# Decay attention and two feed-forward stages: all attention in float32 matmuls, weights P kept for two units

## The chip, the cores and the metric

The kernel runs on one core of a Trainium2 chip. The metric is the device time of one execution in microseconds (us). Three timed runs of the kernel before gave 955.11, 959.03 and 954.88 us, median 955.11.

## What is computed

Causal attention with a decay (4 batches, 8 heads, 576 positions, head dimension 64), then two feed-forward stages over 2304 tokens of width 512, all in float32 accuracy; the weights of the feed-forward stages come as float64.

```python
scores = scale * q @ k.T
cum = cumsum(log(clip(f, 1e-4, 1)))
scores = where(causal, -1e9, scores + cum[:, None] - cum[None, :])
attn = exp(scores - max); attn /= sum(attn) + 1e-9
x = attn @ v                       # then (tokens, 512)
h = x @ w_in;  h = (h * tanh(softplus(h))) @ w_out
out = max(h @ w1, h @ w2, h @ w3) @ w2_out
```

## The kernel before

**Attention by pairs and units.** Two heads make a pair; the 16 pairs run in order, four to a batch. A pair has two units: g = 0 holds query tiles 0 and 1 (128 rows each, 128 and 256 keys wide), g = 1 tiles 2, 3 (384 and 512 wide) and the last 64 rows of both heads together (tile `q4`, twice 288 wide). For a pair, `prep` turns q and k (PE transposes through PSUM tiles `tr`) into `kT` and `qh`. For a unit, `scores` makes a score tile `sc` by matmul; DVE adds the decay `cb` and takes the minimum (line 476), ACT does exp with the sum (482), DVE and POOL scale by the reciprocal (453 to 456). The result is P. Then `av` turns P, 128 x 128 at a time, into PSUM tiles `pp` (510), copies them to TA or TB, multiplies with v into `av` (532 or 539), and writes the result `xt` to DRAM as `x_d` (570).

**Two ways of multiplying.** `WHOLE = 8` sends pairs 0 to 7 through plain float32 matmuls: a score of one head uses the 64 rows of its head (array mode 64*128; `U` and `L` are the two halves), av writes 64 columns for each head (mode 128*64), and q4's scores and all turns use the whole array (128*128). Float32 matmuls appear in the trace as two records each. Pairs 8 to 15 take the split path: q, k, v and P are split into a high and a low float32r part by DVE, ACT and POOL, both parts stand side by side in the contraction, and every matmul uses mode 128*128, two per product (431, 539); q and k are turned in three versions (362), 27 turns for a pair in place of 10.

**PSUM and P.** `tr`, `sc` and `pp` share four PSUM buffers. P has one buffer per tile name.

**Order.** `attention` emits the scores of a unit, then av of the unit before (`pend`), then prep of the next pair. Between units the main loop emits steps of the first feed-forward layer, `h_steps`: 72 steps, 9 blocks of 256 tokens by 8 column groups, each of 24 float32r matmuls (mm3, lines 188 to 190), at a lower priority. A step needs its block's x: `load_x` reads `x_d` back (213) and POOL splits it into xh and xl (142, 146). A scheduler orders each engine's instructions by priority when the kernel is built; on the chip every engine follows that list. What is left of the steps runs after the attention, and then the next layer (`y`, float32r matmuls with w_out) and the second feed-forward stage.

Of the kernel before, what the change touches and what calls it, by code (L numbers as in the profile page):

```python
# [9 lines left out]
F32 = mybir.dt.float32  # L10
F32R = mybir.dt.float32r
# [22 lines left out]
BLK2 = 512  # L34

WHOLE = 8
# [3 lines left out]
PADS = []  # L40
PART0 = [(1, 256, 0, 256)]
# [28 lines left out]
def tile_decay_attention__mish_ff__max3_ff(  # L70
# [39 lines left out]
    with tc.high_priority(3 * AHEAD):  # L110
        make_identity(nc, ident)
        identr = const.tile([128, 128], F32R, name="identr")
        nc.vector.tensor_copy(identr, ident)
# [120 lines left out]
    raws = [ap_.tile([128, 640 if c == "v" else S], F32, name=f"raw{c}") for c in "qkv"]  # L234


    made_for = {}

    def shared(name, whole):

        if made_for.get(name, (None,))[0] != whole:
            dt = F32 if whole else F32R
            if name[:2] == "vs":
                t = aw.tile([128, 10, 2, 64], dt, name=name)
                if whole:
                    t = t.rearrange("p n a d -> p (n a d)")[:, 0:640]
                    nc.gpsimd.memset(t[U, 512:640], 0.0)
            elif name[:2] == "qk":
                t = ap_.tile([128, 9, 3 - int(name[2]), 64], dt, name=name)
                if whole:  # L250
                    t = t.rearrange("p n a d -> p (n a d)")[:, 0:S]
            elif name[:2] == "q4":
                t = as_.tile([128, 2, 256], dt, name=name)
                if whole:
                    t = t[:, 0, 0:128]
                    nc.gpsimd.memset(t, 0.0)
                else:
                    nc.gpsimd.memset(t[:, :, 64:192].bitcast(F32), 0.0)
            else:
                t = aw.tile([128, 2, 768 if name == "TA" else TBW], dt, name=name)  # L260
            made_for[name] = (whole, t)
        return made_for[name][1]

    for t in sums:
        nc.vector.memset(t, 1.0)
    nc.gpsimd.memset(raws[2][U, 512:640], 0.0)
    count = dict(pair=0, prep=0, unit=0, bank=0)

    def ld(dst, src, b, hp, inner):

        hs = slice(2 * hp, 2 * hp + 2)
        if inner:

            nc.sync.dma_start(
                dst[:, 0:512].rearrange("p (h c) -> p h c", h=2),
                src[b, hs, 0:512, :].rearrange("h (p t) d -> p h (t d)", t=4),
            )
            for h in range(2):
                nc.sync.dma_start(dst[(U, L)[h], 512:S], src[b, 2 * hp + h, 512:S, :])
        else:  # L280
            for h in range(2):
                nc.sync.dma_start(
                    dst[:, h * 256:(h + 1) * 256].rearrange("p (t d) -> p t d", t=4),
                    src[b, 2 * hp + h, 0:512, :].rearrange("(t p) d -> p t d", t=4),
                )
            nc.sync.dma_start(
                dst[L, 512:640].rearrange("p (h d) -> p h d", h=2),
                src[b, hs, 512:S, :].rearrange("h p d -> p h d"),
            )

    def split_raw(t, r, eng="dve"):

        split(t[:, :, 0], t[:, :, 1], r.rearrange("p (n d) -> p n d", d=64), eng, "pool")

    def load(b, hp):

        i = count["pair"]
        count["pair"] += 1
        rq, rk, rv = raws
        whole = i < WHOLE  # L300
        if whole:
            if i % 2:
                rq, rk = (shared(f"qk{n}", True) for n in range(2))
            for dst, src in ((rk, k), (rq, q)):
                for h in range(2):
                    nc.sync.dma_start(
                        dst[:, 0:512].rearrange("p (t h d) -> p t h d", h=2, d=64)[:, :, h],
                        src[b, 2 * hp + h, 0:512, :].rearrange("(t p) d -> p t d", t=4),
                    )
                for h in range(2):  # L310
                    nc.sync.dma_start(dst[(U, L)[h], 512:S], src[b, 2 * hp + h, 512:S, :])
        else:
            ld(rk, k, b, hp, True)
            ld(rq, q, b, hp, True)
# [7 lines left out]
        if not whole:  # L322
            ld(rv, v, b, hp, False)
# [3 lines left out]
        return dict(b=b, hp=hp, cb=(c2, c4), raw=(rq, rk), vs=None if whole else shared(f"vs{i % 2}", False), whole=whole)  # L327
# [24 lines left out]
    def prep(J):  # L352

        raw = raws

        qh = as_.tile([128, 2, 512], F32 if J["whole"] else F32R, name="qh", bufs=2)
        kk = as_.tile([128, 2, S], F32 if J["whole"] else F32R, name="kT", bufs=2)
        last = shared(f"q4{count['prep'] % 2}", J["whole"])
        count["prep"] += 1

        def turn(dst, c, src):
            nc.tensor.transpose(dst[:, c:c + 128].bitcast(F32R), src, identr)

        rest = att_psum("tr")
        if J["whole"]:
            kk, qh = kk[:, 0, :], qh[:, 0, :]
            raw = J["raw"]
            for i, dst in ((1, kk), (0, qh)):
                tr = att_psum("tr")
                for c in range(4):  # L370
                    nc.tensor.transpose(tr[:, c * 128:c * 128 + 128], raw[i][:, c * 128:c * 128 + 128], ident)
                nc.scalar.activation(dst[:, 0:512], tr, AF.Copy)
                nc.tensor.transpose(rest[U, i * 128:i * 128 + 128], raw[i][:, 512:S], ident)
            for h, rows in enumerate((U, L)):
                nc.scalar.activation(kk[rows, 512:S], rest[U, 128 + h * 64:192 + h * 64], AF.Copy)
                nc.scalar.activation(
                    last[rows, h * 64:h * 64 + 64], rest[U, h * 64:h * 64 + 64], AF.Copy
                )
            vs = shared(f"vs{(count['prep'] - 1) % 2}", True)
            ld(vs, v, J["b"], J["hp"], False)  # L380
            J.update(q=qh, q4=last, k=kk, vs=vs)
            mask_decay(J)
            return

        ql = as_.tile([128, 2, 512], F32R, name="ql", bufs=2)
        qk = [shared(f"qk{n}", False) for n in range(2)]
        split_raw(qk[1], raw[1])
        split_raw(qk[0], raw[0])
        nc.gpsimd.tensor_scalar(
            qk[0][:, :, 2], raw[0].rearrange("p (n d) -> p n d", d=64), 1.0, 1.0, op0=ALU.mult, op1=ALU.mult  # L390
        )
        for i, part, dst, n in ((1, 0, kk, 0), (0, 0, qh, 1), (0, 1, ql, 2)):
            src = lambda blk: qk[i][:, blk, part:part + 2, :].rearrange("p a d -> p (a d)")
            for h in range(2):
                tr = att_psum("tr")
                for c in range(4):
                    turn(tr, c * 128, src(4 * h + c))
                nc.scalar.activation(
                    dst[:, h, 0:512].rearrange("p (c t) -> p c t", t=4),
                    tr.rearrange("p (t c) -> p c t", t=4),  # L400
                    AF.Copy,
                )
            turn(rest, n * 128, src(8))
        rr = rest[:, 0:384].rearrange("p (i h c) -> p i h c", i=3, h=2)
        nc.scalar.activation(kk[:, :, 512:S], rr[:, 0], AF.Copy)
        for a in range(2):
            nc.scalar.activation(
                last[:, a].rearrange("p (a c) -> p a c", c=64)[:, 0:4:3, :], rr[:, 1 + a], AF.Copy
            )
        split_raw(J["vs"], raw[2], "act")  # L410
        mask_decay(J)
        J.update(q=(qh, ql), q4=last, k=kk)

    def score_mm(J, h, qt, dst, c0, w):
        if J["whole"]:
            if h is None:
                lhs = J["q4"]
                rhs = J["k"][:, c0:c0 + w]
            else:
                lhs = J["q"][(U, L)[h], qt * 128:qt * 128 + 128]  # L420
                rhs = J["k"][(U, L)[h], c0:c0 + w]
            nc.tensor.matmul(dst, lhs, rhs, start=True, stop=True, skip_group_check=True)  # L422
            return
        if h is None:

# [605 lines left out]
```

## Time and profile before

| | before |
|---|---|
| median of 3 runs | 955.11 us |
| the profiled execution | 956.07 us, its span 954.3 us |
| PE / DVE / ACT / POOL busy | 921.3 / 553.8 / 445.5 / 268.5 us |
| mean granted clock of PE | 0.987 |
| first h matmul, last av | 89.0 us, 384.4 us after the span's start |
| last h matmul | 471.7 us |

Times in the trace count from the span's start. A PE row gives the time from a matmul's start to its result; matmuls overlap, so the distance of starts tells what one costs. A record such as `x8` merges neighbours of one kind. `<-` behind a row names what ended the idle time before it. The granted clock is 1.00 at 2.4 GHz and 0.5 at 1.2 GHz.

### The profile page before, as it was taken

To read this page: it belongs to the slowest core of one execution; us is meant where nothing else is said; L and a number is where in the kernel's file an instruction comes from. 1 tells how busy PE (TensorE), PEld (TensorE's weight loads), DVE (VectorE), ACT (ScalarE), POOL (GpSimd) and SP (SyncE) were. 2 spreads that over 40 slices of the span, in tenths; PEclk is the share of its full clock that TensorE was granted. 3 is DMA by queue.
4 is the path that set the end of the run, shared out by engine and by line. 5 is a ranking of instruction groups with operands and counts; after the bars stand their busy time and mean duration, and the time that the engine had idled before them with its cause. 6 is when DMAs were issued, how large, how long until landed. Compare 5 with 4: busy or idle time off the path is not lost.

```text
span 954.3 us, 15673 instructions
## 1 busy us (share of the span) xinstructions
PE 921.3 (97%) x5480; PEld 789.3 (83%) x5480; DVE 553.8 (58%) x1257; ACT 445.5 (47%) x1003; POOL 268.5 (28%) x353
## 2 busy tenths in 40 slices
PE   6899999999999999899999999999999999999998
PEld 3555677799999999799987878789888999789986
DVE  4457787656665556589146656577684446615440
ACT  5567566666666565433245454554443123412221
POOL 3436666574445621210002000000121233103310
PEclk9889999999999999899999999999999999999999
DMA  7757665554445321867255576665399534334311
GB/s 164 182 143 194 206 184 169 162 154 129 130 136 162 115 69 59 300 207 243 95 181 165 186 224 195 224 213 168 127 308 340 159 115 131 105 100 128 116 32 68
DMA packets 131391, 154.81 MB, mean 162 GB/s; under 512 B 52016, under 2 KB 91440, under 8 KB 131312
## 3 DMA queue, kind: packets, MB, share of 16 engines
q1 hardware_dynamic: 108784, 114.48, 40.6%
q10 hardware_dynamic: 19840, 25.17, 7.4%
q0 software_dynamic: 2688, 14.16, 4.1%
q8 instruction: 43, 0.70, 0.3%
q14 instruction: 36, 0.29, 0.1%
HBM read 107.55 MB, written 46.21 MB: 161 GB/s over the span
## 4 chain that ended last, share of the span: by engine, by line
PE 67%; DMA 15%; DVE 7%; ACT 5%; issue 3%; SPq 1%; POOL 1%; ACTq 0%; POOLq 0%; DVEq 0%
DMA g<-h_d 9%; PE h L189 6%; PE h L190 6%; PE h L188 6%; PE q L189 5%; PE q L190 5%; PE q L188 5%; PE pp L510 4%; PE sc L431 3%; PE av L539 3%; DMA wr<-in_moe_w_in_dram 3%; PE o L188 2%; PE o L189 2%; PE o L190 2%; PE sc L422 2%
## 5 line engine op out<-in xcount | busy, mean ns | idle before, releaser
L188 PE MATMUL h<-xh,wi 128*128 128x256 f32 x576 | 167.5, 291 | 4.0 <-POOL xh L142 2.6
L189 PE MATMUL h<-xl,wi 128*128 128x256 f32 x576 | 166.7, 290 | 1.9 <-POOL xl L146 1.9
L190 PE MATMUL h<-xh,wi 128*128 128x256 f32 x576 | 166.5, 289 | 0.0
L189 PE MATMUL y<-gl,wo 128*128 128x512 f32 (+1 forms) x320 | 118.2, 369 | 0.0
L188 PEld LDWEIGHTS h<-xh,wi 128*128 128x128 f32 x576 | 110.5, 192 | 8.6 <-issue 3.1
L190 PE MATMUL y<-gh,wo 128*128 128x512 f32 (+1 forms) x320 | 117.3, 368 | 0.0
L189 PEld LDWEIGHTS h<-xl,wi 128*128 128x128 f32 x576 | 110.8, 193 | 6.6 <-issue 3.1
L190 PEld LDWEIGHTS h<-xh,wi 128*128 128x128 f32 x576 | 110.8, 192 | 2.9 <-issue 2.2
L188 PE MATMUL y<-gh,wo 128*128 128x512 f32 (+1 forms) x320 | 109.3, 371 | 2.8 <-ACT ze L793 2.5
L765 DVE TENSOR_TENSOR gl<-g,gh 128x512 fp32r<-128x512 f32 x72 | 50.3, 699 | 95.4 <-ACT gh L764 94.8
L758 ACT ACTIVATE g<-g 128x512 f32<-128x512 f32 x72 | 45.3, 631 | 89.2 <-DMA g<-h_d 77.4
L482 ACT ACTIVATE P<-P,mn 128x128 f32<-128x128 f32 (+3 forms) x128 | 71.1, 556 | 32.7 <-DVE mn L476 31.6
L188 PEld LDWEIGHTS y<-gh,wo 128*128 128x128 f32 x320 | 60.1, 188 | 15.1 <-ACT ze L793 4.0
L456 POOL TENSOR_SCALAR P<-P,rr 128x128 f32<-128x128 f32 (+3 forms) x128 | 68.3, 548 | 11.9 <-DVE rr L454 6.5
L189 PEld LDWEIGHTS y<-gl,wo 128*128 128x128 f32 x320 | 60.3, 188 | 11.0 <-DVE gl L765 1.3
L190 PEld LDWEIGHTS y<-gh,wo 128*128 128x128 f32 x320 | 60.2, 189 | 9.8
L510 PE MATMUL pp<-ident,P 128*128 128x128 f32 x320 | 60.9, 295 | 6.2 <-POOL P L456 3.7
L957 DVE TENSOR_TENSOR u<-q,p 128x448 f32<-128x448 f32 x36 | 22.4, 622 | 63.6 <-PE q L190 61.2
L510 PEld LDWEIGHTS pp<-ident,P 128*128 128x128 f32 x320 | 41.2, 150 | 16.9 <-issue 6.5
L853 POOL DMA_DIRECT2D r<-a_d x12 | 6.7, 559 | 161.9 <-ACT b L140 161.6
L764 ACT ACTIVATE gh<-g 128x512 fp32r<-128x512 f32 x72 | 44.7, 620 | 14.3 <-PE y L190 13.6
L177 DVE SCALAR_TENSOR_TENSOR wt<-wr,wt 128x512 int32<-128x512 int32 (+1 forms) x62 | 46.9, 756 | 0.6
(178 smaller groups left out, 2138.4 us busy)
## 6 DMA issues: line engine op xcount, KB each, us to landing
g<-h_d SPq DMA_DIRECT2D x72, 256.0 KB, 3.5
s<-s_d SPq DMA_DIRECT2D x72, 256.0 KB, 2.9
h_d<-he ACTq DMA_DIRECT2D x46, 256.0 KB, 3.2
wr<-in_moe_w_out_dram SPq DMA_DIRECT2D x22, 512.0 KB, 4.5
wr<-in_moe_w_dram SPq DMA_DIRECT2D x24, 384.0 KB, 4.3
s_d<-sk POOLq DMA_DIRECT2D x12, 768.0 KB, 5.0
cb<-cum_d SPq DMA_DIRECT2D x32, 256.0 KB, 4.2
wr<-in_moe_w_in_dram SPq DMA_DIRECT2D x32, 256.0 KB, 3.5
```

Of the source, the lines that this page charges most:

```text
L177: nc.vector.scalar_tensor_tensor(out=ti, in0=lo, scalar=29, in1=ti, op0=ALU.logical_shift_right, op1=ALU.bitwise_or,)
L188: nc.tensor.matmul(ps, wh, xh, start=start, stop=False, skip_group_check=True)
L189: nc.tensor.matmul(ps, wh, xl, start=False, stop=False, skip_group_check=True)
L190: return nc.tensor.matmul(ps, wl, xh, start=False, stop=stop, skip_group_check=True)
L431: nc.tensor.matmul(o, lhs, rhs, start=n == 0, stop=n == len(mms) - 1, skip_group_check=True)
L456: nc.gpsimd.tensor_scalar(made[ci], made[ci], rr[:, ci:ci + 1], 1.0, op0=ALU.mult, op1=ALU.mult)
L482: nc.scalar.activation(Pt, Pt, AF.Exp, scale=-1.0, bias=mn[:, col - 1:col], accum_out=sm[:, ci:ci + 1],)
L510: nc.tensor.transpose(pp[:, n * 128:n * 128 + 128], Pt[:, k0:k0 + 128], ident)
L539: nc.tensor.matmul(avp[h][:, off:off + w], vl, T[:, i, c:c + w], start=kt == 0 and i == 0 and not (g == 0 and h == 1), stop=last and i == ...
L758: nc.scalar.activation(g, g, AF.Mish)
L764: on_act[:] = [nc.scalar.activation(gh, g, AF.Copy)]
L765: on_dve[:] = [nc.vector.tensor_tensor(out=gl, in0=g, in1=gh, op=ALU.subtract)]
```

## The change

- The split path, its identity `identr` and the tiles shared between both paths are gone; all 16 pairs take the plain float32 path.
- P has two buffers (`bufs=LEAD`, 2), and av of a unit follows the scores of two more units: `pend` is a list.
- The score tiles of a unit are issued query tile by query tile, head 0 and head 1 next to each other, instead of head by head.
- q and k have two raw buffers for all pairs, v three.

```diff
-WHOLE = 8
+LEAD = 2
...
+    raws = [[ap_.tile([128, S], F32, name=f"raw{c}{i}") for c in "qk"] for i in range(2)]
+    vs = [aw.tile([128, 640], F32, name=f"vs{i}") for i in range(3)]
...
     def prep(J):
...
+        qq = as_.tile([128, 512], F32, name="qT", bufs=2)
+        kk = as_.tile([128, S], F32, name="kT", bufs=2)
+        last, v_ = q4[J["i"] % 2], vs[J["i"] % 3]
         rest = att_psum("tr")
...
-        split_raw(qk[1], raw[1])
-        split_raw(qk[0], raw[0])
...
-        for i, part, dst, n in ((1, 0, kk, 0), (0, 0, qh, 1), (0, 1, ql, 2)):
...
     def score_mm(J, h, qt, dst, c0, w):
...
-            parts = [(t[:, h, qt * 128:qt * 128 + 128], h) for t in J["q"]]
-        mms = [(ql, J["k"][:, n, c0:c0 + w], dst) for ql, n in parts]
-        for n, (lhs, rhs, o) in enumerate(mms):
-            nc.tensor.matmul(
-                o, lhs, rhs, start=n == 0, stop=n == len(mms) - 1, skip_group_check=True
-            )
+            rows = (U, L)[h]
+            lhs = J["q"][rows, qt * 128:qt * 128 + 128]
+        nc.tensor.matmul(dst, lhs, J["k"][rows, c0:c0 + w], start=True, stop=True, skip_group_check=True)
...
-        tiles += [(h, qt) for h in range(2) for qt in ((0, 1) if g == 0 else (2, 3))]
+        tiles += [(h, qt) for qt in ((0, 1) if g == 0 else (2, 3)) for h in range(2)]
...
-            Pt = aw.tile([128, wd], F32, name=f"P{qt}_{h}")
+            Pt = aw.tile([128, wd], F32, name=f"P{qt}_{h}", bufs=LEAD)
...
-                nc.scalar.activation(T[:, 0, cols], src, AF.Copy)
-                nc.vector.tensor_tensor(out=T[:, 1, cols], in0=src, in1=T[:, 0, cols], op=ALU.subtract)
...
+            if count["bank"] % 2:
+                nc.vector.tensor_copy(T[:, c:c + w], pp[:, :w])
+            else:
+                nc.scalar.activation(T[:, c:c + w], pp[:, :w], AF.Copy)
...
-                vl = J["vs"][:, 4 * h + kt if kt < 4 else 8 + h].rearrange("p a d -> p (a d)")
-                for i in range(2):
...
+                n = 4 * h + kt if kt < 4 else 8 + h
+                nc.tensor.matmul(
+                    acc[(U, L)[h], off:off + w], J["vs"][:, n * 64:n * 64 + 64], T[:, c:c + w],
+                    start=kt == 0, stop=last, skip_group_check=True,
+                )
...
     def attention():
...
+        units = [(ji, g) for ji in range(len(jobs)) for g in range(2)]
+        pend = []
+        for n in range(len(units) + LEAD):
+            if n < len(units):
+                ji, g = units[n]
+                pend.append((J[ji], g, scores(J[ji], g)))
+            if n >= LEAD:
+                unit = pend.pop(0)
+                av(*unit)
...
+            if n < len(units):
+                if g == (ji == 0) and ji + 1 < len(jobs):
+                    prep(J[ji + 1])
+                if g == 1 and ji + 2 < len(jobs):
+                    J[ji + 2] = load(ji + 2, *jobs[ji + 2])
+            yield tok
```

The order of PE before, in the plain pair 1 (mode 64*128 for `qh`; 384 and 512 columns of head 0, then of head 1):

```order
L422 MATMUL sc<-kT,q_372 128x288
L422 MATMUL sc<-kT,qh 128x384
L422 MATMUL sc<-kT,qh 128x512
L422 MATMUL sc<-kT,qh 128x384
L422 MATMUL sc<-kT,qh 128x512
L510 MATMUL pp<-ident,P_0_446 128x128
```

There the four scores stand together. The order of PE before, in a split pair (both parts of one head's score, h matmuls between the heads; all in mode 128*128):

```order
L431 MATMUL sc<-kT,q_2560 128x288 x8
L431 MATMUL sc<-kT,qh 128x384
L431 MATMUL sc<-kT,ql 128x384
L188 MATMUL h<-xh,wi_160 128x256
L189 MATMUL h<-xl,wi_160 128x256
L190 MATMUL h<-xh,wi_160 128x256
L431 MATMUL sc<-kT,qh 128x512
L431 MATMUL sc<-kT,ql 128x512
```

The order of PE after the change, in a pair of the second half (`sc` in mode 64*128, `av` in 128*64, h, lines 184 to 186, in 128*128; a row of `sc` is one head's score):

```order
L324 MATMUL sc<-kT,qT 128x128
L403 MATMUL av<-TB,vs_186 64x320 x2
L184 MATMUL h<-xh,wi_156 128x256
L185 MATMUL h<-xl,wi_156 128x256
L324 MATMUL sc<-kT,qT 128x128
L403 MATMUL av<-TB,vs_186 64x320
L186 MATMUL h<-xh,wi_156 128x256
L324 MATMUL sc<-kT,qT 128x256
L403 MATMUL av<-TB,vs_186 64x320 x2
```

Here the two heads' scores of 128 columns are apart, and the mode changes with nearly every row. Over the whole attention 34 stretches of mode 64*128 and 44 of 128*64 become 87 and 101.

The DMA queue of SP at the attention's end, before (`x_d<-xt` are the last units' results, `xr<-x_d` the reads for the next h block; 66 is block 6):

```order
L570 DMA x_d_66<-xt_5190 128x64
L570 DMA x_d_67<-xt_5190 128x192
L213 DMA xr<-x_d_66 128x1024
L639 DMA h_d_7_92<-he 256x1x256
L570 DMA x_d_67<-xt_5336 128x64
L570 DMA x_d_68<-xt_5336 128x256
```

and after:

```order
L209 DMA xr<-x_d_65 128x1024
L307 DMA vs_185<-in_v_dram 128x4x64 x2
L311 DMA vs_185<-in_v_dram 64x2x64
L417 DMA x_d_67<-xt_4151 128x64
L417 DMA x_d_68<-xt_4151 128x256
L417 DMA x_d_66<-xt_4354 128x64
```

Before, block 6 is read right behind the last write to it, and the PE order has 48 h steps ahead of the last av. After the change block 5 is read ahead of the last fourteen writes, and 30.6 h steps stand ahead of the last av.

## Rows read from the trace of the kernel before

**Rows 1.** The page: span, and busy time of each engine.
```profile
span 954.3 us, 15673 instructions
...
PE 921.3 (97%) x5480; PEld 789.3 (83%) x5480; DVE 553.8 (58%) x1257; ACT 445.5 (47%) x1003; POOL 268.5 (28%) x353
```

**Rows 2.** Busy time by stretch: length, then PE, PEld, DVE, ACT, POOL, clock.
```profile
25.00:50.00 25.00, 22.83 (x117) 12.99 (x117) 10.04 (x37) 14.18 (x44) 9.81 (x21) 0.86 0.68 171
50.00:75.00 25.00, 23.86 (x123) 14.28 (x121) 17.33 (x60) 18.22 (x53) 9.39 (x15) 0.86 0.58 156
75.00:100.00 25.00, 23.61 (x135) 15.47 (x135) 16.61 (x52) 16.87 (x52) 18.87 (x28) 0.93 0.78 222
100.00:175.00 75.00, 72.25 (x465) 51.94 (x464) 60.97 (x133) 46.21 (x119) 44.90 (x52) 1.00 0.60 177
200.00:350.00 150.00, 150.00 (x1266) 148.91 (x1265) 88.68 (x267) 94.52 (x239) 76.41 (x105) 1.00 0.43 130
375.00:400.00 25.00, 20.46 (x148) 20.07 (x147) 10.36 (x20) 11.40 (x20) 7.27 (x5) 0.86 0.69 230
```

**Rows 3.** Busy time of tile h's instructions alone, 200 to 350 us.
```profile
200.00:350.00 150.00, 100.13 (x652) 86.20 (x651) 8.94 (x13) 8.36 (x14) 1.00 0.43 130
```

**Rows 4.** PE in order of time, split path: start us, us, then the group.
```profile
188.74 1.57 PE L362 MATMUL tr<-identr,qk 128*128 128x128 f32 x16
...
193.69 0.69 PE L431 MATMUL sc<-kT,q 128*128 128x288 f32 x4
...
195.56 0.39 PE L431 MATMUL sc<-kT,qh 128*128 128x512 f32 x1
195.80 0.40 PE L431 MATMUL sc<-kT,ql 128*128 128x512 f32 x1
```

**Rows 5.** PE in order of time around the last av.
```profile
382.17 2.52 PE L539 MATMUL av<-TB,vs 128*128 128x320 f32 x17
387.30 0.50 PE L188 MATMUL h<-xh,wi 128*128 128x256 f32 x2 [2.61 <-POOL xh L142]
389.72 0.58 PE L189 MATMUL h<-xl,wi 128*128 128x256 f32 x1 [1.93 <-POOL xl L146]
```

**Rows 6.** PE in order of time, plain path, 101 to 122 us.
```profile
101.13 0.76 PE L532 MATMUL av<-TB,vs 128*64 128x320 f32 x4 [0.70 <-ACT TB L523]
101.82 0.66 PE L371 MATMUL tr<-ident,rawk 128*128 128x128 f32 x4
102.40 0.75 PE L532 MATMUL av<-TB,vs 128*64 128x320 f32 x2
103.08 0.30 PE L373 MATMUL tr<-ident,rawk 128*64 128x128 f32 x1
...
109.03 1.12 PE L422 MATMUL sc<-kT,qh 64*128 64x512 f32 x2
110.08 0.39 PE L188 MATMUL h<-xh,wi 128*128 128x256 f32 x1
110.30 0.28 PE L189 MATMUL h<-xl,wi 128*128 128x256 f32 x1
110.51 0.91 PE L422 MATMUL sc<-kT,qh 64*128 64x384 f32 x2
111.35 0.39 PE L190 MATMUL h<-xh,wi 128*128 128x256 f32 x1
...
121.91 0.60 PE L510 MATMUL pp<-ident,P 128*128 128x128 f32 x4
```

**Rows 7.** PE in order of time, both heads' scores with nothing between them.
```profile
52.37 1.81 PE L422 MATMUL sc<-kT,qh 64*128 64x384 f32 x8
54.13 0.52 PE L510 MATMUL pp<-ident,P 128*128 128x128 f32 x3
```

**Rows 8.** What PE waited for, 12 to 100 us: us in total, times, longest.
```profile
PE pp L510 <- POOL P L456: 3.7, 5, 1.6
```

**Rows 9.** PE in order of time, turns of P in a phase of low clock.
```profile
61.53 1.27 PE L510 MATMUL pp<-ident,P 128*128 128x128 f32 x5
```

More of the change, by code (lines that the diff above doesn't have):

```diff
@@ L264, in tile_decay_attention__mish_ff__max3_ff @@
+    raws = [[ap_.tile([128, S], F32, name=f"raw{c}{i}") for c in "qk"] for i in range(2)]
+    vs = [aw.tile([128, 640], F32, name=f"vs{i}") for i in range(3)]
+    TA = aw.tile([128, 768], F32, name="TA")
+    TB = aw.tile([128, TBW], F32, name="TB")
     for t in sums:
         nc.vector.memset(t, 1.0)
[L266 to L276, printed above, removed]
-            )
-            for h in range(2):
-                nc.sync.dma_start(dst[(U, L)[h], 512:S], src[b, 2 * hp + h, 512:S, :])
-        else:
+    q4 = [as_.tile([128, 128], F32, name=f"q4_{i}") for i in range(2)]
@@ L284, in ld @@
                     src[b, 2 * hp + h, 0:512, :].rearrange("(t p) d -> p t d", t=4),
                 )
[L286 to L314, printed above, removed]
@@ L315, in load @@
+                nc.sync.dma_start(dst[(U, L)[h], 512:S], src[b, 2 * hp + h, 512:S, :])
         r = b * H + 2 * hp
@@ L352, in prep @@
     def prep(J):
[L354 to L362, printed above, removed]
-        rest = att_psum("tr")
[L365 to L383, printed above, removed]
@@ L404, in prep @@
[L404 to L410, printed above, removed]
+        b, hp, raw = J["b"], J["hp"], J["raw"]
+        qq = as_.tile([128, 512], F32, name="qT", bufs=2)
+        kk = as_.tile([128, S], F32, name="kT", bufs=2)
@@ new lines, in prep @@
+        last, v_ = q4[J["i"] % 2], vs[J["i"] % 3]
+        rest = att_psum("tr")
+        for i, dst in ((1, kk), (0, qq)):
+            tr = att_psum("tr")
+            for c in range(4):
+                nc.tensor.transpose(tr[:, c * 128:c * 128 + 128], raw[i][:, c * 128:c * 128 + 128], ident)
+            nc.scalar.activation(dst[:, 0:512], tr, AF.Copy)
+            nc.tensor.transpose(rest[U, i * 128:i * 128 + 128], raw[i][:, 512:S], ident)
+        for h, rows in enumerate((U, L)):
+            nc.scalar.activation(kk[rows, 512:S], rest[U, 128 + h * 64:192 + h * 64], AF.Copy)
+            nc.scalar.activation(last[rows, h * 64:h * 64 + 64], rest[U, h * 64:h * 64 + 64], AF.Copy)
@@ L411, in prep @@
+        for h in range(2):
+            nc.sync.dma_start(
+                v_[:, h * 256:(h + 1) * 256].rearrange("p (t d) -> p t d", t=4),
+                v[b, 2 * hp + h, 0:512, :].rearrange("(t p) d -> p t d", t=4),
+            )
+        nc.sync.dma_start(
+            v_[L, 512:640].rearrange("p (h d) -> p h d", h=2),
+            v[b, 2 * hp:2 * hp + 2, 512:S, :].rearrange("h p d -> p h d"),
+        )
+        J.update(q=qq, q4=last, k=kk, vs=v_)
         mask_decay(J)
-        J.update(q=(qh, ql), q4=last, k=kk)
@@ L414, in score_mm @@
     def score_mm(J, h, qt, dst, c0, w):
[L415 to L423, printed above, removed]
         if h is None:
-            parts = [(J["q4"][:, a, n * 128:n * 128 + 128], n) for n in range(2) for a in range(2)]
+            lhs, rows = J["q4"], slice(0, 128)
@@ L494, in av @@
         gw = 256 if g == 0 else 320
+        T = (TA, TB)[g]
         xt = aw.tile([128, gw], F32, name=f"xt{g}")
-        whole = J["whole"]
-        T = shared(("TA", "TB")[g], whole)
-        avt = [aps.tile([128, 512], F32, name="av", bufs=2) for _ in range(2 - (g == 0 or whole))]
-        if whole:
-            avp = [avt[0][U, 0:gw], avt[0][L, 0:gw]]
-        else:
-            avp = [avt[0][:, 0:256], avt[0][:, 256:512]] if g == 0 else [t[:, 0:gw] for t in avt]
+        acc = aps.tile([128, 512], F32, name="av", bufs=2)
         for blocks, products in (LAYA, LAYB)[g]:
@@ L529, in av @@
-            for kt, h, c, off, w, last in products:
-                if whole:
-                    n = 4 * h + kt if kt < 4 else 8 + h
-                    nc.tensor.matmul(
-                        avp[h][:, off:off + w], J["vs"][:, n * 64:n * 64 + 64], T[:, 0, c:c + w],
-                        start=kt == 0, stop=last, skip_group_check=True,
-                    )
-                    continue
-                vl = J["vs"][:, 4 * h + kt if kt < 4 else 8 + h].rearrange("p a d -> p (a d)")
-                for i in range(2):
-                    nc.tensor.matmul(
-                        avp[h][:, off:off + w], vl, T[:, i, c:c + w],
-                        start=kt == 0 and i == 0 and not (g == 0 and h == 1), stop=last and i == 1,
-                        skip_group_check=True,
-                    )
@@ L544, in av @@
[L544 to L564 removed]
+            w, c = len(blocks) * 128, blocks[0][3]
@@ L565, in av @@
+        parts = [(0, 0, 0, gw)]
+        parts += [(1, 0, 256, 64), (1, 64, 128, 128), (1, 192, 0, 128)] if g else [(1, 0, 0, 256)]
+        for h, c, o, w in parts:
+            rows = (U, L)[h]
+            nc.scalar.activation(xt[rows, o:o + w], acc[rows, c:c + w], AF.Copy)
         t0 = J["b"] * S + q0
```

115 lines of the change are left out of this document (16 added, 99 removed).

## The prediction

> **What bounds the kernel now.** I read the page first. The span is 954.3 us [rows 1]; the execution itself took 956.07 us, 0.96 us above the 955.11 us median of the runs shown. Then I read the busy times by stretch [rows 2]: the reader should look at PE against the length of each stretch. From 200 to 350 us PE is busy for 150.00 of 150 us with 1266 matmuls, one per 0.118 us, while DVE has 88.68, ACT 94.52 and POOL 76.41. Between 25 and 100 us PE is still busy for 91 to 95% of the time and no other engine comes near that. So for the whole attention part PE is the bound, and a saving on DVE, ACT or POOL is worth only what PE waits for them. Over the whole span PE is busy for 921.3 us, 97% [rows 1], so it is as full behind the attention, and what PE gains or loses early arrives at the end. The question is therefore how much PE time the old and the new attention take.
>
> PE's durations overlap (a matmul is recorded with 0.28 us but a new one starts every 0.118 us), so I price by starts: from the start of one row to the start of the next.
>
> **The split path that goes.** Eight of the 16 pairs used it. It runs wholly in tile mode 128*128 and shares PE with the h matmuls without a gap: from 200 to 350 us 652 instructions of h [rows 3] at 0.118 us are 77 us, and 73 us are left for about 5.9 pairs (25.3 us a pair), 12.4 us each. By kinds [rows 4]: its 216 turns of q and k are 16 in 1.57 us, the last one's 0.28 us aside 0.086 us each, 18.6 us. Its scores are, per pair, 8 of 256 columns at 0.118, 8 of 288 at 0.136 ((0.69 - 0.28) / 3), 4 of 384 at about 0.18 and 4 of 512 at 0.24 (195.56 to 195.80): 3.7 us, times 8 is 29.6 us. Its 224 av products: 17 in 2.52 us [rows 5], 0.14 us each for the 96 of 320 columns; the 128 narrower ones lie between that and the turns, I take 0.1 us; 26.2 us. Together 74.4 us go, and per pair with the 25 turns of P the sum is 12.1 us, close to the 12.4 us of the stretch.
>
> **What comes in its place.** Rows of the plain path exist, so nothing here has to be guessed [rows 6]:
> - 80 float32 turns of q and k at 0.11 us ((0.60 - 0.27) / 3): +8.8 us.
> - A float32 score of one head costs by its width: 512 columns last from 109.03 to 110.08, 384 from 110.51 to 111.35, so 0.21 us more for 128 columns, 1.65 ns a column, and about 0.2 us besides. A head is 64 rows, half of the array, and two heads can share it: both heads' 384 and 512 columns, 8 records, are over in 1.76 us [rows 7], which is what one head alone needs (0.84 + 1.05). They did so although the order before issues 384 and 512 of one head, then of the other. So putting heads side by side gives nothing that an uninterrupted stretch didn't have; what counts is whether something stands between them. The same with av: two heads of 320 columns take 0.69 us, one takes 0.68 [rows 6].
> - So I counted, in the order of PE before and after, the visits to a half-array mode, and in each visit the columns of the fuller half. Scores: 34 visits become 87, and 14,720 columns that run one after another become 29,696. 63 of the 87 visits hold one head alone, since h matmuls, turns or av products stand between the two. Had all been paired it would be 20,480. av: 44 visits become 101, 14,848 columns become 31,808 (25,600 if all were paired). At 1.65 ns that is +24.7 us for scores and +28.0 us for av. The last 64 rows of both heads (288 columns, whole array) add 16 more: +7.6 us.
> - Each change of mode costs. Entering for scores, the row before lasts 0.21 us (110.30 to 110.51) in place of 0.118; the first h afterwards, 110.08 to 110.30, lasts 0.22; inside, 512 columns take 0.20 us more than 512 x 1.65 ns. That is 0.39 us for a visit, 0.2 us a change. An av visit has 0.69 - 0.53 = 0.16 us inside and some 0.15 around, 0.15 us a change. Two changes a visit, less those from one half-array mode straight into the other (7 + 7 before, 31 + 30 after): 142 become 315. 173 more at 0.17 us: +29.4 us.
>
> PE's sum: 8.8 + 24.7 + 28.0 + 7.6 + 29.4 - 74.4 = **+24.1 us**. The turns of P are 400 in both. The h matmuls too are the same 1728; they only move: 48 of the 72 steps stood ahead of the last av before, 30.6 do now, and the other 41 run after it.
>
> The Trainium skill's "TensorEngine Tiling (Array Packing)", section Key Properties, says that changing the tiling mode drains the engine. Rows 6 agree (0.21 in place of 0.118 us at the entry, and as much at the exit); the page gives no price, so by it alone the sum would have no last term and be -5.3 us.
>
> **Waits.** The longer lead is meant for PE's wait for P. All such waits are small: turns of P behind POOL's scaling wait 3.7 us in all between 12 and 100 us [rows 8]. I take them as gone, -3.7. Behind the last av, h waits 2.61 us for xh and 1.93 us for xl [rows 5], since the next h needs what attention has just written; then PE runs at half its clock (0.86 granted from 375 to 400 us [rows 2] is 7 us at half, less what fell into the wait), some 2.8 us more. After the change h still has its fourth block to do at that point, whose x was written long ago, so both go: -7.3. What is late next: at the very start, the turns of P now follow the scores of the second pair, which need that pair's q and k turned first, with nothing else for PE to do: between 0 and 5 us, I take +2. And the plain pairs with h between them lost a little more than the split ones (100 to 175 us: 72.25 of 75 busy; 200 to 350 us: all), about 1 us in 25 us of wall time; between nothing and 8 us over the eight pairs, I take +3. DVE, ACT and POOL lose work (no subtractions, no splits), hidden before behind PE, so that is worth nothing. The added DMA is smaller packets of q and k for eight pairs, behind a DMA share of 0.43 in that stretch: nothing; if it were not hidden, it would delay turns that come a whole pair later.
>
> Sum: 24.1 - 3.7 - 7.3 + 2 + 3 = +18.1 us on 956.1, **974 us**; against the median, **973 us**.
>
> **The clock** is the open cost. Three of the stretches before 100 us have a granted clock of 0.86, 0.86 and 0.93 [rows 2]; 1.00 being 2.4 GHz, that is 17 us at 1.2 GHz and 8.7 us lost. What PE did there: float32 work and turns alone, no h; in one of these phases the turns of P took 0.21 us each, 5 in 1.27 us [rows 9]. With h between (100 to 175 us) it stayed at 1.00. I keep the 8.7 us of the first four pairs and add none later. Bounds: all of it gone (-8.7), or a phase like these now and then in the later pairs, at 3.4 us each.
>
> **Rivals.**
> - *The lower clock spreads.* The later pairs now are the work during which it fell, with some 70 h in a pair where there were 109. Against it: the plain pairs from 100 to 175 us had no more h and kept 1.00. One phase in every second of twelve pairs is 6 x 3.4 = 20 us: 993 us. Chance 0.13.
> - *No difference.* The lead removes all of PE's idle time from 25 to 175 us (7.4 us by rows 2, where I took 3.7) and with it the low clock (8.7): 973 - 3.7 - 8.7 = 961 us, and 956 without the 5 us of new waits. For it: a steadier PE. Against: PE is already over 90% busy there. Chance 0.08.
> - *Faster, since halves fill up.* If lone visits overlapped with their neighbours, as the two heads did against the order in rows 7, columns would fall to the paired counts, -15.2 and -10.2 us, and with half of the 173 added changes gone, -14.7: 973 - 40 = 933 us. It decides from about 60% of that on. Against it: lone 512 and 384 visits between h matmuls run to their full length in rows 6 with nothing inside. Chance 0.05. The Trainium skill's "TensorE: Matmul & The Clock Gate", Part 3, has small matmuls in different parts of the array run concurrently; by that alone this rival would be the forecast, and rows 6 show why it is not: an h or a turn of the whole array stands between.
> - That heads side by side does nothing is part of the forecast: 24 of the 87 visits hold both.
>
> **How the numbers follow.** The forecast, 962 to 986 us, has 0.74, the rivals 0.13, 0.08 and 0.05. Low end of the range: half of the 8.7, no new waits (-5), mode changes at 0.15 us (-3.5) makes 960 us. High end: the end wait stays (+7.3), new waits at their bounds (+8), two or three clock phases: 996 us. Below 960 lie the rest of the second and the third rival, above 996 the rest of the first; together under 2 in 10. About 0.5%, 4.8 us, is what a measurement of this kernel can tell from no change: faster 0.05, same 0.08, slower 0.87.
>
> **What would show it.** Right: PE still busy for nearly all of 100 to 400 us; a pair of the later ones takes about 15 us of PE beside its h, in place of 12.4; the last av starts near 360 us (before: 384, with 49 us more h ahead of it), some 117 us of h follow, and all later stages are the same but shifted by 15 to 20 us; no wait for xh behind the last av; three dips of the clock before 100 us. Wrong: waits of PE for DVE or ACT in 100 to 360 us of more than 10 us; dips of the clock there; scores with one head in 0.5 us visits, or heads overlapping across an h matmul.

## The result and the profile after the change

The change is slower by about 0.9%: median 963.89 us over 20 runs (960.31 to 970.2) against 955.0 us over 20 runs of the kernel before (949.92 to 962.87), ratio 1.0088, interval 1.0069 to 1.0108, or +8.9 us where +18 was forecast. The time lies inside the range, its direction was the forecast one, and the size was about twice too large.

The page of the kernel after, span and busy time of each engine, against [rows 1]:

```profile
span 960.5 us, 15156 instructions
...
PE 936.5 (97%) x5312; PEld 755.2 (79%) x5312; DVE 506.6 (53%) x1164; ACT 417.6 (43%) x967; POOL 229.1 (24%) x319
```

The span grew by 6.2 us and PE's busy time by 15.2. So PE's idle time, span less busy, fell from 33 to 24 us. DVE, ACT and POOL lost 47, 28 and 39 us of work, and the kernel became no faster for it.

Busy time by stretch in the kernel after; the columns are those of [rows 2]:

```profile
0.00:25.00 25.00, 14.90 (x57) 8.93 (x58) 11.30 (x49) 13.24 (x41) 10.03 (x30) 0.91 0.69 162
25.00:50.00 25.00, 23.68 (x137) 13.71 (x135) 13.98 (x53) 17.87 (x54) 11.84 (x25) 0.95 0.74 179
50.00:75.00 25.00, 24.20 (x148) 13.76 (x147) 15.08 (x57) 18.98 (x61) 11.13 (x23) 1.00 0.75 196
75.00:100.00 25.00, 21.08 (x111) 11.76 (x110) 20.28 (x56) 17.60 (x50) 19.82 (x24) 0.93 0.69 194
100.00:175.00 75.00, 74.73 (x469) 51.74 (x468) 56.40 (x143) 48.53 (x127) 41.62 (x53) 1.00 0.66 199
200.00:350.00 150.00, 150.00 (x969) 106.48 (x971) 58.02 (x202) 73.95 (x214) 46.15 (x76) 1.00 0.35 100
340.00:440.00 100.00, 99.53 (x763) 92.88 (x764) 66.45 (x119) 36.35 (x66) 11.29 (x7) 1.00 0.61 208
```

The same view of the kernel before, for the two stretches that the rows ahead of the prediction don't hold:

```profile
0.00:25.00 25.00, 14.85 (x65) 8.11 (x66) 11.79 (x49) 13.38 (x42) 10.16 (x30) 1.00 0.73 165
340.00:440.00 100.00, 94.08 (x729) 91.73 (x728) 65.96 (x150) 48.51 (x102) 20.35 (x21) 0.97 0.52 172
```

Three things are to be seen. From 200 to 350 us PE is full in both, but it starts 969 matmul records where it started 1266 (a float32 matmul is two of them): that is the added cost, fewer and dearer instructions in the same time. From 340 to 440 us PE was idle for 5.9 us before and is now for 0.5, at a clock of 1.00 in place of 0.97: the wait behind the last `av` is gone. And from 50 to 75 us, where PE does nothing but float32 work in both kernels, the granted clock is 1.00 where it was 0.86.

PE in order of time in the kernel after, a pair of the second half (start us, us, then the group):

```profile
212.62 0.91 PE L324 MATMUL sc<-kT,qT 64*128 64x384 f32 x2
213.46 0.38 PE L186 MATMUL h<-xh,wi 128*128 128x256 f32 x1
213.68 0.28 PE L184 MATMUL h<-xh,wi 128*128 128x256 f32 x1
213.80 0.28 PE L185 MATMUL h<-xl,wi 128*128 128x256 f32 x1
...
214.72 0.91 PE L324 MATMUL sc<-kT,qT 64*128 64x384 f32 x2
215.56 0.38 PE L186 MATMUL h<-xh,wi 128*128 128x256 f32 x1
...
216.23 1.13 PE L324 MATMUL sc<-kT,qT 64*128 64x512 f32 x4
217.28 0.38 PE L184 MATMUL h<-xh,wi 128*128 128x256 f32 x1
```

The 384 columns of the two heads stand apart: each visit takes 0.84 us (212.62 to 213.46, and 214.72 to 215.56). The 512 columns of both heads happen to stand together and take 1.05 us (216.23 to 217.28), what one head alone took in [rows 6]. So a visit that holds one head costs the price of two. The first h after a visit takes 0.22 us (213.46 to 213.68), the next one 0.12. The Trainium skill's "TensorEngine Tiling (Array Packing)", section Key Properties, has a change of the tiling mode drain the engine; these rows agree, with 0.10 us for the change behind a visit.

What PE waited for in the kernel after (us in total, times, longest), the largest of the attention:

```profile
PE tr L300 <- DMA rawk<-in_k_dram: 4.8, 1, 4.8
PE pp L394 <- DVE mn L366: 3.8, 6, 1.6
PE sc L324 <- ACT qT L301: 3.0, 2, 2.5
PE sc L324 <- DVE mn L366: 1.9, 2, 1.4
PE av L403 <- ACT TA L400: 1.7, 3, 1.3
```

The wait for POOL's P of [rows 8] is gone, as is the one for xh and xl of [rows 5]. The turns wait for DVE's minimum for 3.8 us: since `tr`, `sc` and `pp` share four PSUM buffers, most likely for a buffer from which DVE has yet to read a score.

### The profile page after: what moved, and what is told of

Read it like the earlier page. It is cut to its first block, busy times and chain, and to the rows that moved or that the text cites. A ratio compares the mean times of both kernels' runs of the same rounds, so it can differ in the third digit from the quotient of the medians.

```text
span 960.5 us, 15156 instructions
## 1 busy us (share of the span) xinstructions
PE 936.5 (97%) x5312; PEld 755.2 (79%) x5312; DVE 506.6 (53%) x1164; ACT 417.6 (43%) x967; POOL 229.1 (24%) x319
## 4 chain that ended last, share of the span: by engine, by line
PE 75%; DMA 12%; ACT 5%; DVE 4%; issue 3%; SPq 1%; POOL 0%; ACTq 0%; POOLq 0%; DVEq 0%
DMA g<-h_d 9%; PE sc L324 8%; PE h L184 7%; PE h L186 7%; PE h L185 7%; PE av L403 7%; PE q L185 5%; PE q L184 5%; PE q L186 5%; PE pp L394 4%; PE o L184 2%; PE o L185 2%; PE o L186 2%; PE y L184 2%; PE y L186 2%
## 5 line engine op out<-in xcount | busy, mean ns | idle before, releaser
L184 PEld LDWEIGHTS h<-xh,wi 128*128 128x128 f32 x576 | 109.7, 190 | 12.7 <-issue 10.0
L347 POOL TENSOR_SCALAR P<-P,rr 128x128 f32<-128x128 f32 (+3 forms) x128 | 70.6, 565 | 58.4 <-DVE rr L345 38.6
L324 PE MATMUL sc<-kT,qT 64*128 64x128 f32 (+3 forms) x256 | 78.6, 503 | 3.4 <-ACT qT L301 3.0
L403 PE MATMUL av<-TB,vs 128*64 128x320 f32 (+2 forms) x320 | 60.9, 394 | 0.1
L394 PE MATMUL pp<-ident,P 128*128 128x128 f32 x320 | 56.7, 284 | 0.5 <-DVE mn L366 0.5
L324 PEld LDWEIGHTS sc<-kT,qT 64*128 64x128 f32 x256 | 31.8, 197 | 29.0 <-issue 10.3
L486 ACT ACTIVATE he<-h 128x512 f32<-128x512 f32 x46 | 27.3, 594 | 58.1 <-PE h L186 55.6
```

Source lines behind the costliest of these rows:

```text
L184: nc.tensor.matmul(ps, wh, xh, start=start, stop=False, skip_group_check=True)
L324: nc.tensor.matmul(dst, lhs, J["k"][rows, c0:c0 + w], start=True, stop=True, skip_group_check=True)
L347: nc.gpsimd.tensor_scalar(made[ci], made[ci], rr[:, ci:ci + 1], 1.0, op0=ALU.mult, op1=ALU.mult)
L394: nc.tensor.transpose(pp[:, n * 128:n * 128 + 128], Pt[:, k0:k0 + 128], ident)
L403: nc.tensor.matmul(acc[(U, L)[h], off:off + w], J["vs"][:, n * 64:n * 64 + 64], T[:, c:c + w], start=kt == 0, stop=last, skip_group_check= ...
L486: nc.scalar.activation(he, h, AF.Copy)
```

## The experiments

**How the profiles are compared.** A span is split in three. PE's idle time is the part of the span without a matmul. The loss to the clock is half of the time for which PE was busy in the phases of 1.2 GHz. The rest is work, PE's time as it would be at 2.4 GHz. Before the clock first rises, half of PE's busy time counts as work; the other half, 3.5 to 6.6 us in each kernel, is in none of the three columns. Beside it stands what the prediction's method counts: visits, columns of the fuller half and changes of mode in each kernel's PE order, times the same prices of rows 4 to 7, here done for every row of the order. "One head" are the score visits that hold a single head, of all score visits. Spans, idle time, clock and work are of one profile each. Each ratio is against runs of the kernel before taken beside that kernel's own, with medians of 955.0 to 958.1 us, so it does not follow from the first column.

| kernel | median us | ratio to before (interval) | span | idle | clock | work | work, less that of after | counted | one head |
|---|---|---|---|---|---|---|---|---|---|
| before | 955.0 | | 954.3 | 32.9 | 11.0 | 905.8 | -21.1 | -27.0 | 23 of 34 |
| after | 963.89 | 1.0088 (1.0069 to 1.0108) | 960.5 | 24.0 | 4.7 | 926.9 | 0 | 0 | 63 of 87 |
| e1_plain | 987.66 | 1.0327 (1.0288 to 1.0366) | 986.1 | 30.2 | 8.4 | 943.5 | +16.6 | +16.3 | 88 of 98 |
| e2_plain_heads | 979.38 | 1.0231 (1.0196 to 1.0267) | 978.1 | 21.5 | 11.7 | 939.9 | +13.0 | +14.9 | 84 of 98 |
| e3_after_byhead | 969.1 | 1.0126 (1.0087 to 1.0164) | 965.3 | 25.0 | 3.1 | 933.3 | +6.4 | +7.5 | 80 of 92 |
| e5_av_glued | 961.28 | 1.0053 (1.003 to 1.0077) | 959.1 | 32.0 | 7.4 | 914.2 | -12.7 | -12.0 | 68 of 90 |
| e6_both_glued | 965.71 | 1.0087 (1.0057 to 1.0117) | 965.6 | 53.1 | 17.4 | 891.6 | -35.3 | -36.3 | 26 of 70 |
| e7_scores_glued | 984.66 | 1.0287 (1.0249 to 1.0324) | 984.9 | 55.9 | 17.5 | 905.0 | -21.9 | -21.8 | 28 of 69 |
| e8_glued_lead1 | 975.14 | 1.0205 (1.017 to 1.0241) | 972.2 | 62.1 | 17.7 | 888.9 | -38.0 | -39.3 | 0 of 57 |
| e9_glued_from6 | 945.27 | 0.9864 (0.9819 to 0.991) | 946.2 | 35.3 | 7.4 | 899.4 | -27.5 | -30.6 | 26 of 69 |
| e10_glued_from4 | 955.24 | 0.9975 (0.9949 to 1.0002) | 956.8 | 40.8 | 16.3 | 894.6 | -32.3 | -31.6 | 26 of 68 |
| e11_glued_from8 | 943.97 | 0.9869 (0.9839 to 0.9899) | 942.2 | 26.9 | 6.0 | 905.2 | -21.7 | -21.2 | 34 of 73 |

**One part of the change at a time.** e1_plain is the kernel before with all pairs on the plain path, lead and order of heads as before:

```diff
-WHOLE = 8
+WHOLE = 16
```

> All pairs plain, lead of one unit and heads one after the other as before. PE's slots, counted in its order with the prices of the prediction, are 16 us more than in the changed kernel (88 score visits with one head, 35,840 columns in a row) and 43 us more than before. Theory A (PE's work decides; the lead only removes the wait behind the last av, which is gone here too since 35.5 h steps stand ahead of the last av): 964 + 16 = 980 us. Theory B (the longer lead also keeps PE from waiting and the clock from falling before 100 us, some 10 us, which this kernel pays again): 990 us, with two or three dips of the clock before 100 us. Theory C (plain matmuls cost less than I priced them): under 972 us.

Measured: +3.3%, 987.66 us, near theory B; work +37.7 us over the kernel before. e2_plain_heads adds to it the heads side by side:

```diff
-        tiles += [(h, qt) for h in range(2) for qt in ((0, 1) if g == 0 else (2, 3))]
+        tiles += [(h, qt) for qt in ((0, 1) if g == 0 else (2, 3)) for h in range(2)]
```

> As e1_plain, with the two heads of a query tile next to each other. The count is 1.4 us less than e1_plain (84 single visits, 34,688 columns), 15 us more than the changed kernel. Theory A: 979 us. Theory B: 989 us. If putting the heads side by side is worth more than the count says, it is clearly under e1_plain, by 5 us or more.

Measured: 979.38 us, 8.3 us less than e1 by the medians. By the two profiles work fell by 3.6 us and idle time by 8.7, and the clock went the other way by 3.3; so the order of heads was worth more than the count says, and took away more waiting than work. e3_after_byhead is the kernel after with that line undone:

> The changed kernel with the score tiles head by head again. The count is 7.5 us above the changed kernel (80 single score visits instead of 63, 34,304 columns instead of 29,696). By the count 971 us; if the order of heads does nothing on the chip, 964 us. Theory B also wants the clock before 100 us as in the changed kernel.

Measured: 1.0126 against 1.0088, some 3.6 us slower than the kernel after (the two intervals overlap); work +6.4 where 7.5 was counted. So the order of heads is worth something with either lead: with h between, heads that stand apart in the order lose the shared visit.

From e2 to the kernel after the longer lead is left (with the buffers that it needs, and with the loads of q and k in another order). Spans: -17.6 us; work -13.0, clock -7.0, idle +2.5. Nearly three quarters of what the lead gives is thus no wait at all: with two more units of scores ahead of it, `av` falls elsewhere in the order and the score visits that hold one head fall from 84 to 63. The split path with the longer lead alone was not tried.

Busy time of e1_plain from 50 to 75 us, the same columns:

```profile
50.00:75.00 25.00, 19.57 (x90) 10.74 (x89) 19.54 (x51) 15.80 (x44) 11.66 (x16) 0.73 0.53 151
```

The same row of e2_plain_heads:

```profile
50.00:75.00 25.00, 21.86 (x109) 12.55 (x110) 18.62 (x62) 18.58 (x55) 10.72 (x16) 0.86 0.55 148
```

The same row of e3_after_byhead:

```profile
50.00:75.00 25.00, 23.51 (x144) 13.52 (x144) 14.26 (x53) 18.34 (x58) 11.78 (x25) 1.00 0.70 189
```

The two kernels with the short lead have clocks of 0.73 and 0.86 here, the one with the long lead 1.00, whatever the order of heads. None of the three has an h matmul in this stretch.

**Are single profiles enough for that?** Each kernel was profiled once more.

> The kernel before once more, for its clock. If the low clock before 100 us belongs to the kernel, there are again two to four dips of 3.4 or 6.8 us, 14 to 20 us at 1.2 GHz; if it falls by chance, under 10 us or over 24 us. The wait for xh behind the last av is there again with 4 to 5 us.

> The changed kernel once more, for its clock. If the longer lead is what keeps the clock up before 100 us, there are again at most two dips, 10 us or less at 1.2 GHz (before: 17 and 14 us); if its first profile was a lucky one, 14 us or more. No wait for xh behind the last av.

The kernel before lost 10.2 us to the clock (11.0 in the first profile), the kernel after 2.6 (4.7). Before 100 us that is 8.2 and 6.2 against 4.7 and 2.6: 3.5 us less in either pair. Work repeats to 0.4 us, idle time to about 3. The timed runs agree: the mean granted clock is 0.996 in the median of the 20 runs of the kernel after and 0.988 in that of the 52 runs of the kernel before taken beside the experiments, a loss of 3.8 against 11.5 us (the share below 1.00, times the span).

**What the added work is: visits with one head.** A visit of one head costs as much as one of both. If that is right, keeping the heads together must return the work as counted. A matmul of head 0 may start sooner than that of head 1, because what it needs is there sooner; a scheduler that sees this puts h between. e5_av_glued makes `av` of head 0 wait for the copy that head 1 waits for, so that nothing is gained by starting it alone; e6_both_glued adds the same for scores (head 0 waits until DVE has read the score before it, so that both heads find a free PSUM buffer); e7_scores_glued has the scores' part only; e8_glued_lead1 is e6 with the short lead. The excerpt is from e6; e5 has its part on `av` (`PRODB` and `copied`), e7 that on scores (`taken`):

```diff
...
-PRODB = [(kt, h, 640 * kt + 320 * h, 0, 320, False, 5 * kt + (3, 5)[h]) for kt in range(3) for h in range(2)]
+PRODB = [(kt, h, 640 * kt + 320 * h, 0, 320, False, 5 * kt + 5) for kt in range(3) for h in range(2)]
...
+    def behind(mm, first):
+        tc.add_manual_dep(mm.ins, first.ins.name, ...)
...
+                copied = nc.vector.tensor_copy(T[:, c:c + w], pp[:, :w])
...
+                mm = nc.tensor.matmul(acc[(U, L)[h], off:off + w], ...)
+                if h == 0:
+                    behind(mm, copied)
...
+                mm = score_mm(J, h, qt, sc[:, :w], c0, w)
+                if h == 0 and taken:
+                    behind(mm, taken[0])
+                taken[:] = [nc.vector.tensor_tensor_reduce(...)]
```

> The changed kernel, with the av product of head 0 made to wait for the copy that head 1's product waits for, so that both are issued together: 10 av visits with one head instead of 35, 27,392 columns in a row instead of 31,808, 283 changes of mode fewer by about 30. The count is 12 us less: 952 us. If lone visits cost less than priced, or the later start makes PE wait, 960 us or more.

> e5_av_glued, and in addition the score of head 0 waits until DVE has taken the score before it, so that both heads' scores find free PSUM buffers and are issued together: 26 score visits with one head instead of 63, 22,144 columns in a row instead of 29,696, and fewer changes of mode. The count of PE's slots is 36 us below the changed kernel. If PE's work decides: 928 us. Rival: the scores now come in steps of DVE's reduction (about 1 us for two heads), and in the first four pairs, where no h stands in between, PE waits for them some 0.7 us twice a unit, 11 us, and the clock falls as often as before: 940 us. Over 955 us both fall.

> The scores glued as in e6, av as in the changed kernel. The count is 22 us below the changed kernel: 942 us by PE's work alone, up to 953 with the waits of the rival above.

> e6 with a lead of one unit and one buffer for P, as before the change. The count is 3 us below e6. If the longer lead is worth nothing once PE has enough other work: 925 us, or e6 less 3 us. If it is what hides the chain from score to P: e6 plus 7 us or more, with turns of P waiting for POOL and DVE before 100 us, and more time at the low clock.

Measured: work falls by 12.7, 35.3, 21.9 and 38.0 us where 12.0, 36.3, 21.8 and 39.3 were counted. The price of a lone visit is therefore shown. The two parts of the price can be told apart too: work in the eleven plain kernels of the table, fitted to the columns and the changes of mode in each trace's order, gives 1.68 ns a column (standard error 0.19) and 0.16 us a change (0.03), where the prediction took 1.65 and 0.17 from rows. But no kernel here beats the one before, and all four took longer than their counts allowed, since the later starts made PE wait: e5 as its rival said (over 960 us), e6 and e7 far beyond theirs (955 and 953 us). e8 came out 9.4 us above e6, as expected if the longer lead hides the way from score to P. e6 gains 35 us of work and loses 29 to idle time and 13 to the clock. Busy time by stretch of e6:

```profile
25.00:50.00 25.00, 15.67 (x83) 8.67 (x83) 10.40 (x37) 10.86 (x33) 8.80 (x18) 0.79 0.69 178
50.00:75.00 25.00, 20.92 (x115) 13.14 (x115) 18.50 (x57) 19.76 (x59) 15.74 (x23) 0.87 0.60 158
100.00:175.00 75.00, 66.64 (x454) 50.91 (x453) 51.04 (x136) 45.87 (x125) 44.38 (x52) 0.93 0.63 183
200.00:350.00 150.00, 148.65 (x1100) 119.09 (x1100) 55.74 (x198) 72.20 (x212) 53.04 (x86) 1.00 0.45 131
```

and what PE waits for in it:

```profile
PE sc L331 <- DVE mn L375: 13.7, 15, 2.2
PE av L412 <- ACT TB L409: 6.5, 1, 6.5
...
PE tr L307 <- DVE mn L375: 4.7, 4, 1.8
```

Most of the loss stands before 175 us, where PE is idle for 41.9 us in e6 and for 16.4 in the kernel after; from 200 to 350 us PE is idle for 1.35 us and starts 1100 records in place of 969. Early there is no h to run while a glued matmul waits (the first h of e6 starts after 100 us), so its wait is PE's.

**Keeping the heads together only where h fills the wait.** The same edit, for pairs from number 6, 4 and 8 on:

```diff
-                if h == 0 and taken:
+                if h == 0 and taken and J["i"] >= GLUE:
...
-                if h == 0:
+                if h == 0 and J["i"] >= GLUE:
```

> e6_both_glued with the glue only from pair 6 on, where PE has h matmuls to put in while a score waits for DVE. e6 had 35 us less PE work than the changed kernel, as counted, but 29 us more idle time and 13 us more lost to the low clock, nearly all of it before 175 us. The count here is 31 us below the changed kernel. If the waits belong to the pairs without h: idle and clock as in the changed kernel, 933 to 938 us, faster than both kernels. If the glue makes PE wait wherever it stands: 950 us or more, with waits of scores for DVE after 175 us.

> The same from pair 4 on, about where the first h stand. The count is 1 us below e9. If h in between is what pays for the glue, and pairs 4 and 5 still have little of it (the weights of h are being converted by DVE until about 165 us), it comes out 3 to 10 us above e9, with the idle time between 90 and 175 us; if not, 1 us below.

> The glue from pair 8 on. The count is 21 us below the changed kernel and 9 us above e9. e9 still had 9 us of idle time between 90 and 175 us, where the changed kernel had 2. If those belong to pairs 6 and 7, they go, and with them the two dips of the clock there (3 us): 943 to 948 us, level with e9. If they come from the later start of h alone, it is 9 us above e9: 954 us.

Measured: 0.9864, 0.9975 and 0.9869. From pair 6 or 8 on, the kernel is faster than the one before by 1.3 to 1.4% and than the changed one by about 2%; from pair 4 on, idle time and clock take most of it back. e9's own forecast of 933 to 938 us was missed: it stood idle for 35.3 us, not for the 24.0 of the kernel after. e10 and e11 came out where the first case of their expectations put them. Busy time by stretch of e11:

```profile
50.00:75.00 25.00, 24.19 (x149) 14.11 (x149) 14.02 (x57) 18.59 (x59) 11.59 (x24) 1.00 0.71 192
100.00:175.00 75.00, 75.00 (x482) 54.48 (x482) 53.94 (x136) 45.87 (x121) 41.54 (x54) 0.97 0.69 199
200.00:350.00 150.00, 150.00 (x1111) 120.78 (x1109) 57.00 (x196) 68.73 (x202) 51.44 (x82) 1.00 0.40 116
```

It keeps the early stretches of the kernel after and the 1100 records of e6: work as low as that of the kernel before (905.2 against 905.8), without its waits (idle 26.9 against 32.9) and with half its loss to the clock.

## Why the prediction was right in sign and twice too large

By spans (+6.2 us), with each of the prediction's terms:

| term | forecast | measured |
|---|---|---|
| PE's work | +24.1 | +21.1 |
| waits ahead of 340 us: P gone -3.7, start +2, later pairs +3 | +1.3 | -1.2 |
| wait and clock behind the last `av`, to 520 us | -7.3 | -6.4 idle, -2.8 clock |
| clock before 100 us | 0 | -3.4 |
| later stages, and the time before the clock's first rise | 0 | -1.0 |
| sum (of unrounded terms) | +18.1 | +6.2 |

PE's work set the time, as forecast; the sum came out too high because all five terms erred the same way. The largest miss is the clock before 100 us, which the prediction kept as it was (3.4 us); then come PE's work (3.0), the waits (2.5), the end (2.0) and the rest (1.0).

- **PE bounds the attention, and the change adds PE work: right, and shown.** PE is full from 200 to 350 us and starts fewer matmuls. A pair of the second half takes 14.1 us of PE beside its h (432 records of h at 0.118 us and seven pairs, by 175 turns of P, in the 150 us), where about 15 was forecast. The count holds to about 3 us for all plain kernels. Against the kernel before, the full count is high by 5.9 us for the kernel after, by 7.8 for e2 and 5.6 for e1; what these three have in common is the split path's price and that of the turns and q4, so the first was most likely set too low, by up to some 6 us of 74 (the stretch from 200 to 350 us alone had 12.4 us a pair where the prices added up to 12.1). How much of the 6 us belongs to which is not shown. The prediction's own sum missed by only 3, because its coarser columns and changes of mode erred the other way.
- **"Putting heads side by side gives nothing that an uninterrupted stretch didn't have": true of an uninterrupted stretch, not of this kernel.** With h between, e1 to e2 gains 8.3 us and e3 to the kernel after 3.6.
- **New waits, "+2" at the start and "+3" in the later pairs: the first came, the second did not.** At the start the scores of the second pair wait 2.54 us for its turned q. From 0 to 25 us PE is busy for 14.90 us, before for 14.85, but that is not the same work: after the fall of the clock at 20.6 us, 3.6 of the 14.90 us ran at half speed. At full clock it is 8.3 us of work where it was 10.3, so 2 us were lost; the table has nearly all of them under the clock. In the second profiles, where the fall came later, the loss stands as idle time, 1.85 us. The same row of p_before_again and of p_after_again:

```profile
0.00:25.00 25.00, 14.97 (x65) 8.04 (x65) 12.02 (x49) 13.50 (x42) 10.02 (x30) 1.00 0.71 165
0.00:25.00 25.00, 13.12 (x58) 8.23 (x59) 11.39 (x51) 12.98 (x41) 9.64 (x30) 0.95 0.70 163
```

  In the later pairs PE's idle time fell from 2.75 to 0.27 us between 100 and 175 us, and from 175 to 340 us there is none in either kernel. The wait for P went, yet from 25 to 100 us PE is idle for 6.0 us where it was 4.7 (in the second profiles 4.4 where it was 6.0): between 12 and 175 us the turns' wait for DVE's minimum grew from 1.7 to 3.8 us.
- **"I keep the 8.7 us of the first four pairs": the step that failed most plainly.** It was argued from float32 work and turns alone, with no h, but the three falls of the kernel before became two, a gain of 3.4 us. That cause is refuted: from 50 to 75 us the kernel after, e3 and e11 do float32 work alone and have 1.00. The next candidate is the waits. PE in order of time around the first two of these falls in the kernel before (at 40.4 and 57.5 us; the wait stands in brackets):

```profile
38.96 0.44 PE L532 MATMUL av<-TA,vs 128*64 128x128 f32 x4
40.99 0.48 PE L510 MATMUL pp<-ident,P 128*128 128x128 f32 x1 [1.59 <-POOL P L456]
...
55.02 0.44 PE L510 MATMUL pp<-ident,P 128*128 128x128 f32 x2 [0.26 <-DVE mn L476]
...
57.29 0.99 PE L532 MATMUL av<-TA,vs 128*64 128x256 f32 x4
```

  and around the two falls in the kernel after, at 20.6 and 95.7 us:

```profile
21.42 1.65 PE L324 MATMUL sc<-kT,qT 64*128 64x128 f32 x8 [2.54 <-ACT qT L301]
...
95.50 0.33 PE L394 MATMUL pp<-ident,P_None 128*128 128x128 f32 x1 [1.65 <-DVE mn L366]
95.66 0.80 PE L394 MATMUL pp<-ident,P 128*128 128x128 f32 x3
96.26 0.42 PE L394 MATMUL pp<-ident,P_None 128*128 128x128 f32 x1
96.47 0.42 PE L394 MATMUL pp<-ident,P 128*128 128x128 f32 x1
```

  The clock falls with the wait of 1.59 us in the one, and with those of 2.54 and 1.65 in the other (turns 0.11 us apart become 0.21: 96.26 is followed by 96.47). In the two profiles of each kernel 8 of the 12 falls stand in or right behind waits of PE of 1.5 us or more, 3 behind waits of 0.5 to 1.0 us, and ahead of the one at 57.5 us there is none over 0.3 us. Conversely e3 is idle for longer before 100 us than the kernel before (17.2 against 14.9 us), and its clock falls once, at 22.3 us; its wait of 1.63 us at 89.0 us brought no fall:

```profile
90.64 0.44 PE L403 MATMUL av<-TA,vs 128*64 128x128 f32 x4 [1.63 <-ACT TA L400]
```

  So most falls stand at waits, but neither a wait nor the sum of the waits decides. The two kernels with the longer lead lose less to the clock than those with the same order of heads and the short one (4.7 against 11.7 us, e3 3.1 against e1's 8.4); why they do is open.
- **The end: right, a little too small.** The last `av` starts at 352.5 us (forecast near 360), no h waits behind it, and both the idle time and the fall of the clock at 388.6 us are gone: -9.2 in place of -7.3.

```profile
350.99 1.73 PE L403 MATMUL av<-TB,vs 128*64 128x320 f32 x14
352.65 0.39 PE L184 MATMUL h<-xh,wi 128*128 128x256 f32 x1
```

- **The rivals.** The clock did not spread. "No difference" took the right terms, waits and clock, but only a part of each came. "Faster, since halves fill up" does not happen by itself: 63 of 87 score visits hold one head. It happens when the order is made to: the work of e8, which has no lone score visit, falls by 38.0 us where that rival said 40, and e9 and e11 turn a part of it into time.

In medians the change costs 8.9 us, 2.7 more than in the two profiles; single runs of the kernel before lie from 950 to 963 us, and the profiled executions happened to stand 1.1 us above the median of the one kernel (956.07) and 1.6 below that of the other (962.3). That is all of the 2.7.

## What to carry to other kernels

Where one engine is full, count its work from the order it will run and prices read from rows: here that held to about 3 us among the eleven kernels on the plain path, while waits and the clock were the uncertain part. Before saving work by making instructions wait for each other, look at what else the engine has to run at that place: the same edit saved 35 us of work and lost 42 to waits and clock when it covered all pairs, and gained about 2% on the changed kernel when it began where h fills the wait. And price a longer lead by more than the wait it is meant for: it also moves what stands between instructions that belong together, and here the clock stood higher with it, for a reason that these runs leave open.

## What the runs showed of the hardware

- Both halves of the array run at the same time on float32 work, at no cost for the second: 512 columns of both heads in 1.05 us (216.23 to 217.28), as one head alone in [rows 6]. In [rows 7] they did so although the order issues 384 and 512 of one head ahead of 384 of the other: the trace has all four records of 384 columns start (52.37 to 52.81 us) before the first of 512 (53.12 us), and the stretches at 33 and 70 us look alike. So matmuls on different halves do not always start in the order of the list that the engine is given.
- The granted clock can stay at 1.00 through 25 us of float32 matmuls and turns alone (50 to 75 us in the kernel after, e3 and e11), and fell to half in the same kind of work of the kernel before.
- A change of the array's mode costs time of its own, 0.16 us in the mean by the fit over eleven kernels, and the first h behind a score visit takes 0.22 us where the next takes 0.12.
